# Two thirds of one weight row sent through few partitions, one bias load, and four small operations on ScalarE, in a one-core decode kernel

## The chip, the cores and the metric

The kernel runs on one core of a Trainium2 chip. The metric is the device time of one execution in microseconds (us). The time before is the median of three runs.

## What is computed

Two tokens (B = 2, one position each, D = 576) go through an attention block over a cached context and through a dense MLP, and a sigmoid gate mixes the two results. Everything is fp32.

```python
B, Sq, D = 2, 1, 576;  H, Sk, Dh = 32, 4096, 128;  F = 4608
q = (x @ wq) per head
scores = einsum(q, k_cache) * Dh ** -0.5
o = softmax(scores) @ v_cache
a = o.reshape(B, Sq, H * Dh) @ wo
h = gelu(x @ w1 + b1);  b = h @ w2 + b2
g = sigmoid((x * gate_w).sum(-1))
out = g * a + (1 - g) * b
```

`k_cache` and `v_cache` are 134 MB each; the four weight matrices hold some 40 MB. All of it is read once.

## The kernel before, in words

**Storage.** One SBUF tile, `ring` (128 partitions x 49152 floats), takes every large transfer. It has three slots of 16384 floats. `wq` and `w1` come first and lie one behind the other from the start of the ring; behind them lie small temporaries. Then come, slot after slot, K and V of sixteen units (a unit is four heads of one token: 128 partitions x 64 KB), and then three groups of `w2` and `wo`, listed in `LAST` (lines 66 to 70). SyncE (SP) issues all of these in one order that is fixed in `seq` (lines 100 to 104); `load()` and `load_next()` issue the next one when its slot is free. A transfer over 128 partitions is cut into one piece for each partition.

**Start.** SP issues `wq` and `w1` (L119). ScalarE (ACT) issues the MLP's bias `b1` (L218), the two rows of `x` (L223) and `gate_w` (L224), and later `b2` (L314). TensorE transposes `x` (L270), makes the gate (L279) and the projection by `wq` (L303). ACT copies the projection to SBUF (L313), and TensorE gathers the heads (L328); then the first slot is free for the first K (L130). `q_unit` (L343) spreads the queries of four units over 128 partitions with POOL (L347), TensorE (L351) and ACT (L353).

**The MLP's hidden layer.** `w1`'s projection (L303 again) leaves token 0 and token 1 in rows 0 and 1 of each group of 32 partitions. `b1` is loaded twice, once for each of the two rows, by `load_b1`: for token 0 in one transfer ahead of `x`, for token 1 in five transfers behind `b2` (L315), each over 4 partitions. It is added ahead of the transpose (L390). GELU follows, and `hg` (128 partitions x 36 rows x 2 tokens) holds the result times the gate.

**The sixteen units.** VectorE (DVE) multiplies K by the query in place (L506) and sums over the head's 128 elements (L511, L512, with POOL adding halves in L510); the softmax runs on ACT (L531), and TensorE multiplies by V (L545). `keep` and `combine` (L556, L562) collect the results in `oall`.

**The end.** Row r of `w2` on partition p is row 36p + r of the matrix, and row r of `wo` on partition p is 32p + r. `mlp_out` and `wo_out` multiply row after row into one PSUM tile, `acc`, which has two halves of 288 columns (DS) for each of two parities of the row (`acc_mm`, L363). One half of `w2`'s last row, r = 35, is handled apart: its columns 288 to 575 are not in the transfer over 128 partitions (L158). They come as "wx", in four transfers over 4 partitions each (L155), so that 16 partitions hold 8 pieces each, one for each of the 128 places. `hx` holds the matching 128 values of `hg` in that layout (made by eight matmuls, L411, and one copy, L415), and `mlp_x` (L417) multiplies them. The wx transfers are issued between `w2` and `wo`. `wo` comes in pieces of 8, 8, 7, 4, 3, 1 and 1 rows, the last row in three parts (L166). After row 22 `acc` is copied to SBUF (L446); the rows from 23 on go to a second PSUM tile, `res` (L457, L481), in four column quarters, and `fold` adds the copied sums (L467). DVE and ACT copy `res` to SBUF (L477, L486), and SP writes the output (L487).

Between the last attention product and `wo_out` stands a short chain: the sum of the softmax weights (L570), reciprocal, the sum over `oall` and a scaling (L572 to L575, DVE), a transpose (L579, TensorE) and its copy (L580, DVE), `o_turn`'s transposes (L433, DVE), its matmul (L435) and its copy `oP` (L436, DVE).

What orders the DMAs: SP issues in program order. A transfer waits for its slot's readers. The framework also has eight semaphores that the transfers of SP and ACT take in turn, so that a transfer waits until the eighth one before it has landed.

## Time and profile before

| what | value |
|---|---|
| median of 3 runs | 721.74 us (721.65 to 721.84) |
| the profiled execution | 721.61 us |
| its span, from first to last instruction | 719.7 us |
| read from HBM | 308.59 MB, 429 GB/s over the span |
| granted TensorE clock, mean | 0.658 |
| DVE, PE, POOL, ACT busy | 511.8, 216.2, 145.0, 40.0 us |

The profile comes from one execution, 0.13 us below the median of the runs. Its times are us from the start of the span. The profiled time is 1.9 us above the span; that part lies outside what the trace shows. "PE" is TensorE's matmuls, "PEld" its weight loads; "SPq" and "ACTq" are DMA issues by SyncE and ScalarE. In the rows by windows, the two last columns are the share of the 16 DMA engines' time that packets took, and GB/s. A packet is counted whole in the window in which it starts, so a short window can show a share above 1. In the rows of DMA queues, q1 is what SP issues, q10 what ACT issues, and q8 and q14 are instruction fetches; the columns are packets, MB, and share of the 16 engines' time in the window.

### The profile page before, as it was taken

To read this page: it belongs to the slowest core of one execution; us is meant where nothing else is said; L and a number is where in the kernel's file an instruction comes from. 1 tells how busy PE (TensorE), PEld (TensorE's weight loads), DVE (VectorE), ACT (ScalarE), POOL (GpSimd) and SP (SyncE) were. 2 spreads that over 40 slices of the span, in tenths; PEclk is the share of its full clock that TensorE was granted. 3 is DMA by queue.
4 is the path that set the end of the run, shared out by engine and by line. 5 is a ranking of instruction groups with operands and counts; after the bars stand their busy time and mean duration, and the time that the engine had idled before them with its cause. 6 is when DMAs were issued, how large, how long until landed. Compare 5 with 4: busy or idle time off the path is not lost.

```text
span 719.7 us, 3881 instructions
## 1 busy us (share of the span) xinstructions
PE 216.2 (30%) x1647; PEld 62.6 (9%) x1647; DVE 511.8 (71%) x136; ACT 40.0 (6%) x156; POOL 145.0 (20%) x35
## 2 busy tenths in 40 slices
PE   0665022040515050404032140505050503113195
PEld 0322000010101010101000010101010100000032
DVE  0004969779695969596969879696959695988910
ACT  0110010100001010101010100001010101010000
POOL 2000130404050403022040404040503122040400
PEclk9977556575756575566657575657575665757599
DMA  9999999999999999999999999999999999999997
GB/s 409 412 446 427 423 452 415 459 416 452 423 437 424 444 426 430 442 430 441 433 431 437 430 426 444 427 437 437 437 427 448 419 434 433 430 441 434 417 424 310
DMA packets 7278, 308.85 MB, mean 429 GB/s; under 512 B 830, under 2 KB 1362, under 8 KB 1628
## 3 DMA queue, kind: packets, MB, share of 16 engines
q1 hardware_dynamic: 7204, 308.55, 99.2%
q8 instruction: 13, 0.21, 0.1%
q10 hardware_dynamic: 56, 0.05, 0.0%
q14 instruction: 5, 0.04, 0.0%
HBM read 308.59 MB, written 0.00 MB: 429 GB/s over the span
## 4 chain that ended last, share of the span: by engine, by line
DMA 47%; DVE 35%; PE 15%; ACT 1%; issue 1%; ACTq 1%; POOL 0%; DVEq 0%; SPq 0%; POOLq 0%
DMA ring<-in_A_k_cache_dram 38%; DVE ring L506 19%; DVE s L511 10%; PE av L545 10%; DVE s L512 5%; DMA ring<-in_B_w_dram 4%; DMA ring<-in_A_wo_dram 3%; DMA ring<-in_gate_w_dram 3%; PE oall L562 2%; PE qps L303 2%; PE acc L367 1%; DVE avs L556 1%; ACTq L218 0%; PE qps L328 0%; ACT p L531 0%
## 5 line engine op out<-in xcount | busy, mean ns | idle before, releaser
L506 DVE TENSOR_TENSOR ring<-ring,q 128x16384 f32<-128x16384 f32 x16 | 275.6, 17225 | 109.1 <-DMA ring<-in_A_k_cache_dram 109.1
L510 POOL TENSOR_TENSOR ring<-ring 128x3968 f32<-128x3968 f32 x16 | 137.0, 8565 | 490.1 <-DVE ring L506 490.1
L545 PE MATMUL av<-ring,p 128*32 128x512 f32 x1024 | 137.5, 698 | 166.9 <-ACT p L531 166.9
L511 DVE TENSOR_REDUCE s<-ring 128x66 f32<-128x8448 f32 x16 | 143.3, 8953 | 1.3
L562 PE MATMUL oall<-avs,pick 128*64 128x512 f32 x16 | 14.8, 1028 | 196.7 <-DVE avs L556 168.3
L512 DVE TENSOR_REDUCE s<-ring 128x62 f32<-128x3968 f32 x16 | 68.4, 4277 | 0.1
L545 PEld LDWEIGHTS av<-ring,p 128*32 128x32 f32 x1024 | 35.1, 127 | 274.8 <-issue 217.8
L531 ACT ACTIVATE p<-s,bs 32x128 f32<-32x128 f32 x64 | 25.5, 398 | 478.9 <-DVE bs L525 477.7
L351 PE MATMUL qb<-qm,spread 64*128 64x512 f32 x8 | 8.3, 1138 | 72.5 <-POOL qm L347 72.5
L390 DVE TENSOR_TENSOR ring<-hps,ring 128x384 f32<-128x384 f32 x3 | 1.7, 559 | 33.3 <-PE hps L303 33.1
L562 PEld LDWEIGHTS oall<-avs,pick 128*64 128x64 f32 x16 | 2.2, 196 | 203.5 <-DVE avs L556 203.5
L367 PE MATMUL acc<-ring,hg 128*2 128x288 f32 x142 | 11.9, 487 | 26.1 <-DMA ring<-in_B_w_dram 26.1
L283 DVE TENSOR_SCALAR gb<-gb 128x2 f32<-128x2 f32 x1 | 0.2, 170 | 24.7 <-ACT gb L282 24.7
L556 DVE TENSOR_TENSOR avs<-av,selr 128x512 f32<-128x512 f32 x8 | 5.5, 682 | 10.6 <-PE av L545 10.6
L303 PE MATMUL hps<-ring 128*32 128x384 f32 x120 | 12.8, 598 | 0.0
L347 POOL TENSOR_TENSOR qm<-qall,mine 64x512 f32<-64x512 f32 x4 | 4.1, 1032 | 41.7 <-ACT qall L330 41.7
L477 DVE COPY ring<-res 2x144 f32<-2x144 f32 x1 | 0.3, 297 | 16.4 <-PE res L457 16.4
L531 ACT ACTIVATION_READ_ACCUMULATOR p<-s,bs 32x1 f32 x64 | 11.8, 184 | 0.0
L303 PE MATMUL qps<-ring 128*32 128x512 f32 x80 | 11.3, 729 | 0.0
L270 PE MATMUL xps<-ident,ring 3*128 3x3 f32 x10 | 1.5, 254 | 24.0 <-DMA ring<-in_gate_w_dram 23.1
L351 PEld LDWEIGHTS qb<-qm,spread 64*128 64x128 f32 x8 | 2.0, 307 | 75.6 <-POOL qm L347 75.6
L353 ACT COPY q<-qb 128x512 f32<-128x512 f32 x4 | 2.3, 586 | 106.3 <-PE qb L351 106.3
(87 smaller groups left out, 74.3 us busy)
## 6 DMA issues: line engine op xcount, KB each, us to landing
ring<-in_B_w_dram SPq DMA_DIRECT2D x2, 4608.0 KB, 34.4
ring<-in_B_w_dram SPq DMA_DIRECT2D x2, 4032.0 KB
ring<-in_A_wo_dram SPq DMA_DIRECT2D x2, 2304.0 KB, 14.9
ring<-in_B_w_dram SPq DMA_DIRECT2D x1, 2160.0 KB
ring<-in_A_wo_dram SPq DMA_DIRECT2D x1, 2016.0 KB
ring<-in_B_w_dram SPq DMA_DIRECT2D x1, 1152.0 KB, 14.7
ring<-in_A_wo_dram SPq DMA_DIRECT2D x1, 1152.0 KB
ring<-in_A_wq_dram SPq DMA_DIRECT2D x1, 1024.0 KB
```

The source lines that it names most:

```text
L303: nc.tensor.matmul(ps[32 * j:32 * j + 32, :width], lhs, ts[c][:, o:o + width], start=(k == 0), stop=last, skip_group_check=True,)
L347: nc.gpsimd.tensor_mul(t, qall.unsqueeze(1).to_broadcast([NO, NQ, DH]), mine[:, u[0]:u[-1] + 1].unsqueeze(2).to_broadcast([NO, NQ, DH]),)
L351: nc.tensor.matmul(ps, spread, t.rearrange("p u d -> p (u d)"), start=True, stop=True)
L367: nc.tensor.matmul(acc[o:o + m], lhsT, rhs[:, (s - lo) * DS:(s - lo + 1) * DS], start=start, stop=stop, skip_group_check=True)
L506: nc.vector.tensor_mul(kt[i], kt[i], qs[i].unsqueeze(1).to_broadcast([P, R, DH]))
L510: nc.gpsimd.tensor_add(t[:, :, :DH2], t[:, :, :DH2], t[:, :, DH2:])
L511: nc.vector.tensor_reduce(st[i][:, HALVED:], kt[i][:, HALVED:], AX.X, ALU.add)
L512: nc.vector.tensor_reduce(st[i][:, :HALVED], t[:, :, :DH2], AX.X, ALU.add)
L531: nc.scalar.activation(p[w, :, e * RB:(e + 1) * RB], st[i][w].rearrange("p (t c) -> p t c", c=RB), AF.Exp, bias=bias[i][w], accum_out=rs[w ...
L545: nc.tensor.matmul(ps[32 * j:32 * j + 32], p[:, 32 * t + EB * (1 - half):32 * t + EB * (1 - half) + 32], vt[i][:, RB * t:RB * (t + 1)].rea ...
L556: nc.vector.tensor_mul(t, avs[i].rearrange("p (r d) -> p r d", d=DH), selr.unsqueeze(2).to_broadcast([P, RB, DH]))
L562: nc.tensor.matmul(oall, pick[:, NO - G - i * G:2 * NO - G - i * G], avs[i].rearrange("p r d -> p (r d)"), start=(i == 0), stop=(i == N // ...
```

## The change

- **wx is wider and lies differently.** It takes 512 columns (64 to 575) of `w2`'s row 35 in place of 288, so that L158's transfer (now L166) has 224 columns less on each partition. Of the 128 places, 120 come in four transfers over 6 partitions with 5 places each (2 KB pieces), and the last 8 in a fifth transfer over 4 partitions with 2 places each.
- **`mlp_x`** has 7 steps in place of 8, and each has two matmuls (224 and 288 columns) in place of one of 288. `acc_mm` is written for any range of columns. `hx` is made in two parts (5 + 2 matmuls, two copies).
- **`wo` is cut** 7, 7, 9, 4, 3, 1, 1, since the second group has less room in its slot. The assertion is new, and checks that.
- **`b1` is loaded once**, in three transfers over 4 partitions, to row 2 of each group of 32, ahead of `x` on ACT's queue. The five transfers behind `b2` are gone. After the transpose one DVE addition adds that row to both tokens.
- **Four small operations go from DVE to ACT:** the copies of `spread`, `oT` and `oP`, and the scaling of `osum`.

```diff
-        (("w2", 28, 36), ("wx", 0, 1), ("wo", 0, 8), ("wo", 8, 16)),
-        (("wo", 16, 23), ("wo", 23, 27), ("wo", 27, 30), ("wo", 30, 31), ("wo", 31, 32)),
+        (("w2", 28, 36), ("wx", 0, 1), ("wo", 0, 7), ("wo", 7, 14)),
+        (("wo", 14, 23), ("wo", 23, 27), ("wo", 27, 30), ("wo", 30, 31), ("wo", 31, 32)),
...
-    XE, XC = 4, 4
+    XE, XC, XS, XW = 6, 4, 5, 512
     XP = XE * XC
-    XS = P // XP
-    srcx2 = w2.rearrange("(e c s r) n -> c r e s n", e=XE, c=XC, s=XS)[:, NF - 1, :, :, DS:]
+    XN = XP * XS
+    XR, XT = 4, (P - XN) // 4
+    XL = D - XW
+    srcw = w2.rearrange("(p r) n -> p r n", r=NF)[:, NF - 1, XL:]
+    srcx2 = srcw[:XN].rearrange("(e c s) n -> c e s n", e=XE, c=XC)
...
-                xt = t[:XP, o:o + XS * DS]
+                xt = t[:XP, o:o + XS * XW]
                 for c in range(XC):
                     nc.sync.dma_start(xt[c::XC].rearrange("e (s n) -> e s n", s=XS), srcx2[c])
+                o += XS * XW
+                yt = t[:XR, o:o + XT * XW].rearrange("p (s n) -> p s n", s=XT)
+                nc.sync.dma_start(yt, srcw[XN:].rearrange("(p s) n -> p s n", s=XT))
...
-    load_b1(0, (0, F4))
+    for m in range(FB):
+        nc.scalar.dma_start(
+            b1r.rearrange("(g q) n -> g q n", g=NG)[:, B, m * FC:(m + 1) * FC],
+            b1.rearrange("(g n) -> g n", g=NG)[:, m * FC:(m + 1) * FC],
+        )
...
-    load_b1(1, (0, 232, 464, 696, 928, F4))
...
-    nc.vector.tensor_copy(
+    nc.scalar.copy(
         spread.rearrange("p (e c) -> p e c", e=E), row4.unsqueeze(2).to_broadcast([NO, E, PE_])
     )
...
-    hb = ht[:, :, :B]
+    hb = temp(NF * B).rearrange("p (r b) -> p r b", b=B)
+    nc.vector.tensor_add(hb, ht[:, :, :B], ht[:, :, B:B + 1].to_broadcast([P, NF, B]))
...
     def mlp_x():
-        for s in range(XS):
-            acc_mm(hx[:, s], rows["wx"][:, s], s, lo=1)
+        for s in range(XS + XT):
+            acc_mm(hx[s], rows["wx"][s], s, lo=XL)
...
-        nc.vector.tensor_copy(oP.rearrange("p b c -> p (b c)"), ps)
+        nc.scalar.copy(oP.rearrange("p b c -> p (b c)"), ps)
...
-        nc.vector.tensor_scalar_mul(osum, osum, f[:, 0:1])
+        nc.scalar.mul(osum, osum, f[:, 0:1])
```

Where the order of instructions moves, on SP at the end of the program. The rows are transfers, `in_B_w_dram` being `w2`, with their shape and what the issue waits for; a wait named DMAHW is for an earlier transfer's landing. Before:

```order
L158 DMA ring<-in_B_w_dram 128x4320 [waits DMAHW5_49,DVE_49]
L155 DMA ring<-in_B_w_dram 4x8x288 [waits DMAHW6_49]
L155 DMA ring<-in_B_w_dram 4x8x288 x3
L166 DMA ring<-in_A_wo_dram 128x4608
L166 DMA ring<-in_A_wo_dram 128x4608 [waits DMAHW7_49]
L166 DMA ring<-in_A_wo_dram 128x4032 [waits DMAHW0_49,PE_49]
L166 DMA ring<-in_A_wo_dram 128x2304 [waits DMAHW1_49,PE_49]
L166 DMA ring<-in_A_wo_dram 128x1728 [waits DMAHW2_49,PE_49]
```

And after, the same stretch:

```order
L166 DMA ring<-in_B_w_dram 128x4096 [waits DMAHW2_49,DVE_49]
L157 DMA ring<-in_B_w_dram 6x5x512 x4
L160 DMA ring<-in_B_w_dram 4x2x512 [waits DMAHW3_49]
L174 DMA ring<-in_A_wo_dram 128x4032 [waits DMAHW4_49]
L174 DMA ring<-in_A_wo_dram 128x4032 [waits DMAHW5_49]
L174 DMA ring<-in_A_wo_dram 128x5184 [waits DMAHW6_49,PE_49]
L174 DMA ring<-in_A_wo_dram 128x2304 [waits DMAHW7_49,PE_49]
L174 DMA ring<-in_A_wo_dram 128x1728 [waits DMAHW0_49,PE_49]
```

With one transfer more ahead of them, each of the `wo` transfers waits for the landing of the transfer eight before it, and that is now one later in the list of `w2` than before: the second piece waits for rows 14 to 27 of `w2`, and the third for rows 28 to 35.

On ACT at the start of the program, its first twelve rows, up to the second copy of the projection (L313, now L319) and what follows it. `in_B_b_dram` is `b1` in the rows with 4 partitions and `b2` in the row 1x576. Before (the next two rows are the last of the five `b1` transfers and the copies at L322):

```order
L218 DMA ring<-in_B_b_dram 4x1152
L223 DMA ring<-in_A_x_dram 1x576 x2
L224 DMA ring<-in_gate_w_dram 1x576
L261 ACT_TABLE_LOAD
L261 COPY ring<-ring 3x64 x2
L273 COPY ring<-xps 128x10x2
L275 COPY ring<-xps 128x5
L282 ACTIVATE gb<-zps 128x2
L313 COPY ring<-qps_150 128x512
L313 COPY ring<-qps_151 128x512
L314 DMA ring<-in_B_b_dram 1x576
L218 DMA ring<-in_B_b_dram 4x232 x4
```

After:

```order
L224 DMA ring<-in_B_b_dram 4x384 x3
L229 DMA ring<-in_A_x_dram 1x576 x2
L230 DMA ring<-in_gate_w_dram 1x576
L267 ACT_TABLE_LOAD
L267 COPY ring<-ring 3x64 x2
L279 COPY ring<-xps 128x10x2
L281 COPY ring<-xps 128x5
L288 ACTIVATE gb<-zps 128x2
L319 COPY ring<-qps_152 128x512
L319 COPY ring<-qps_153 128x512
L320 DMA ring<-in_B_b_dram 1x576
L327 COPY ring<-ident 128x4x2 x8
```

Two transfers more stand ahead of `x` and `gate_w`, and five fewer ahead of the copies at L322 (now L327).

## The prediction

> **What bounds the kernel now.** I begin with the page: is any engine full? DVE is busy for 71% of the span, the DMA engines for all of it, and the rows of the queues say what they carry.

> ```profile
> DMA  9999999999999999999999999999999999999997
> q1 hardware_dynamic: 7204, 308.55, 99.2%
> q8 instruction: 13, 0.21, 0.1%
> ```

> The DMA view for the first 710 us alone gives a sharper figure, and the rows by windows show that no stage is an exception:

> ```profile
> q1 hardware_dynamic: 6394, 306.44, 99.8%
> ...
> 2.00:36.00 34.00, 11.51 (x72) 5.55 (x76) 1.75 (x9) 2.09 (x6) 2.47 (x8) 1.00 0.96 413
> 36.00:45.75 9.75, 6.46 (x52) 3.33 (x40) 0.00 (x0) 2.07 (x10) 0.00 (x0) 0.88 0.98 422
> 110.00:650.00 540.00, 139.63 (x912) 34.08 (x904) 437.92 (x91) 29.18 (x115) 122.88 (x17) 0.62 1.00 433
> 690.00:712.00 22.00, 17.79 (x229) 6.35 (x223) 2.64 (x9) 0.43 (x1) 0.00 (x0) 1.00 1.00 425
> ```

> So SP's transfers keep all 16 engines at work from the start to 710 us. At 425 GB/s and share 1.00 one engine moves 26.6 GB/s. The long waits of the chain (K landing, 38% of the span) are this one limit seen from DVE. What is left to ask is how the work is spread over the 16 engines, since the last one to finish sets the end. The windows at the end answer that:

> ```profile
> 713.00:713.50 0.50, 0.19 (x8) 0.18 (x12) 0.00 (x0) 0.13 (x1) 0.00 (x0) 1.00 0.99 394
> 713.50:714.00 0.50, 0.50 (x24) 0.44 (x20) 0.00 (x0) 0.00 (x0) 0.00 (x0) 1.00 0.95 374
> 714.00:714.50 0.50, 0.50 (x24) 0.35 (x16) 0.00 (x0) 0.00 (x0) 0.00 (x0) 1.00 0.78 303
> 714.50:715.00 0.50, 0.22 (x8) 0.00 (x0) 0.00 (x0) 0.00 (x0) 0.00 (x0) 1.00 0.59 214
> 715.00:715.50 0.50, 0.14 (x8) 0.13 (x11) 0.00 (x0) 0.00 (x0) 0.00 (x0) 1.00 0.52 194
> 715.50:716.00 0.50, 0.50 (x24) 0.40 (x16) 0.00 (x0) 0.00 (x0) 0.00 (x0) 1.00 0.46 158
> 716.00:716.50 0.50, 0.50 (x22) 0.17 (x12) 0.00 (x0) 0.00 (x0) 0.00 (x0) 1.00 0.47 119
> 716.50:717.00 0.50, 0.50 (x15) 0.24 (x12) 0.10 (x1) 0.06 (x1) 0.00 (x0) 1.00 0.00 0
> ```

> The engines do not end together. At 713.5 all work; by 715 the share is 0.52, so eight (0.52 x 16) are through; the other eight run on to about 716.5. That is a spread of some 3 us. The chain of waits confirms that this decides:

> ```profile
> 695.27 20.04 DMA ring<-in_A_wo_dram
> ...
> 715.36 1.56 PE res L457 x36
> 716.92 0.28 DVE ring L477
> ```

> From 695 us on the chain is a `wo` transfer until 715.3, complete only when its slowest engine is, and then 1.56 us of matmuls. The pieces after it land on the same slow engines. **The step to cost is therefore: by how much does the slowest of 16 engines move?**

> **The change, part by part.** *The w2 row over 128 partitions.* Each partition has 224 columns, 896 bytes, less. An engine serves 8 of the 128 partitions, so each has 7168 bytes less: 0.27 us at 26.6 GB/s.

> *wx.* Before, four transfers bring 128 pieces of 1152 bytes; on four engines, as the four partitions suggest, that is 32 x 1152 = 36864 bytes each. After, if six partitions mean six engines, each of these gets 4 x 5 pieces of 2048 bytes = 40960, and four of them 2 pieces more = 45056. So per engine: the four old ones 45056 - 36864 - 7168 = +1024 bytes, 0.04 us, which ten packets fewer may take back: 0. Two new ones +33792 bytes: 1.27 us at 26.6 GB/s, or 1.57 at the 21.5 that a busy engine still makes of the small last pieces (158 GB/s at share 0.46); I take 1.3, as 2 KB pieces are longer than those. The other ten: -0.27.

> [...]

> *b1.* The five transfers behind `b2` disappear; at the start 4608 bytes for each of four partitions come as before, in three pieces. ACT's queue in the window that holds the five, and instruction fetches for comparison, here one in a window of 1 us:

> ```profile
> q10 hardware_dynamic: 41, 0.02, 1.1%
> ...
> q8 instruction: 1, 0.02, 6.3%
> ```

> 1.1% of 16 engines over the 6 us from 44 to 50 is 1.06 us for the 41 packets, `b2`'s included, so at most 0.26 us on each of four engines; less the two additional pieces at the start I take 0.2. As the queue never empties, an engine that is relieved at 45 us is still ahead at 716.

> The other row prices one fetch of 16 KB: 6.3% x 16 x 1.0 us = 1.0 us on one engine. Thirteen of them over a few engines make engines late that have nothing to do with wx. Of the eight late ones four are explained by wx and the rest by these.

> *ACT at the start.* These rows of the timeline tell when things are needed:

> ```profile
> 23.07 0.60 PE L270 MATMUL xps<-ident,ring 3*128 3x3 f32 x4 [23.07 <-DMA ring<-in_gate_w_dram]
> 39.79 2.65 ACTq L218 DMA_DIRECT2D ring<-in_B_b_dram  x5
> 42.74 3.01 PE L328 MATMUL qps<-ring 128*64 128x128 f32 x16 [3.29 <-ACT ring L322]
> 45.75 0.33 SPq L130 DMA_DIRECT2D ring<-in_A_k_cache_dram  x1
> ```

> `gate_w` lands fourth in ACT's queue at 23.0 and will land sixth. The first four took 21 us, some 5 each, because each of their packets takes its turn behind a 64 KB piece of `wq`; those pieces end at about 22 us (8 x 64 KB at 26.6 GB/s are 19.7 us, begun at 2), and 8 KB pieces follow. So the two transfers more cost 1 to 2 us, at most 10.5. Against that, 2.65 us of issues leave the path between the projection and L328. The first K would be issued about 1 us earlier than 45.75. Nor is it urgent: `wq` and `w1` are 20.05 MB, of which at 45.75 some 1.9 MB are still to come (34 us at 413 GB/s and 9.75 at 422 have passed), over 4 us of work. Cost 0.

> *GELU's addition and hx.* One DVE addition (0.2 us) delays `hg` and the K that waits for it at 69 us, while a whole V (8.4 MB, 19 us at 433 GB/s) is still queued ahead of it: 0.

> *SP at the end.*

> ```profile
> 681.76 0.33 SPq L158 DMA_DIRECT2D ring<-in_B_w_dram  x1
> 685.40 15.23 SPq L166 DMA_DIRECT2D ring<-in_A_wo_dram  x9
> ```

> wx is issued between these rows, four transfers in 2.8 us; a fifth makes `wo`'s first piece 0.7 us later. The second piece then waits for `w2`'s rows 14 to 27 and the third for rows 28 to 35, which land near 690 and 695 us. By 695 the first two `wo` pieces, 14 rows or 4.1 MB, are still queued: 9.7 us of cover. What the fifth could hold up is the `wo` issues behind it on SP, and none is due. Cost 0.

> *PE and the moved operations.*

> ```profile
> L575 DVE TENSOR_SCALAR ring<-ring 64x128 f32<-64x128 f32 x1 | 0.3, 277 | 0.0
> L580 DVE COPY oT<-oT_t 128x64 f32<-128x64 f32 x1 | 0.2, 225 | 1.5 <-PE oT_t L579 1.5
> L436 DVE COPY oP<-op_t 128x64 f32<-128x64 f32 x1 | 0.2, 224 | 1.8 <-PE op_t L435 1.8
> ...
> 705.82 2.12 PE L367 MATMUL acc<-ring,oP 128*2 128x288 f32 x32 [1.58 <-DMA ring<-in_A_wo_dram]
> 710.57 2.11 PE L367 MATMUL acc<-ring,oP 128*2 128x288 f32 x28 [2.63 <-DMA ring<-in_A_wo_dram]
> 713.31 1.16 PE L457 MATMUL res<-ring,oP 128*2 128x144 f32 x32 [0.63 <-DMA ring<-in_A_wo_dram]
> 715.36 1.51 PE L457 MATMUL res<-ring,oP 128*2 128x144 f32 x36 [0.64 <-DMA ring<-in_A_wo_dram]
> ```

> If ACT took twice as long for each of the three, that is 0.7 us, against 1.58 us in which PE sits waiting for `wo` afterwards; `spread` is covered by POOL's 1 us of L347. `mlp_x` goes from 16 to 28 matmul passes, under 1 us more at the 2.1 us that 16 took, in the same cover; if both bounds came together, 0.1 us would spill into the next gap of 2.63. The piece that lands at 710.5 now has 9 rows, not 7: 8 passes more at 2.11/28 = 0.6 us, which just fills the 0.63 at 713.31, with 0.64 more at 715.36. Cost 0; if the cover were gone, 0.6.

> **Sum.** The late engines: those of wx get 0.2 us less (b1), the others 0.27 less. All `wo` landings of the slowest engine move by about -0.25 us, and what follows them stays. The profiled 721.61 us become 721.36; the median, 0.13 above it, 721.74 becomes 721.5. That is -0.03%. The measurement tells 0.2% from no change, 1.44 us, so this counts as the same.

> **The rivals.**
> 1. *The relief doesn't arrive.* The windows show when engines finish, not which, and a fetch of 1 us can fall on another engine, since PE's program changes by a few instructions. Then 721.7. Chance 0.13.
> 2. *An additional wx engine is one of the late ones.* It adds 1.3 us to an engine that is at most 0.3 us ahead of the last: 722.7 to 723.0. Of the 12 engines without wx, eight are early and four late; knowing no more, both new ones are early with 8/12 x 7/11 = 0.42. But following the packets by hand through the records, end to start (no view lists them by engine), the q8 fetches come back to the same engines and spare those of wx and the early ones beside them. [...] Chance of the rival 0.12.
> 3. *Slower: six partitions don't give six engines.* If the transfers went over two, each would get 4 x 3 x 5 x 2048 = 122880 bytes, 86016 more than before: 3.2 us less 0.27. If those two are among the late, the end is at 724.6; it decides once an engine gets more than the 3 us of spread. For it: no such shape in the trace. Against: four partitions evidently use more than two. Chance 0.03.
> 4. *Slower: `x` late.* If the two transfers cost 10.5 us, the first K comes 7.9 us later, the queue is empty for 3.5, and nothing gives that back: 725.2. It decides from 7 us on (4.4 of cover and 2.65 saved). Against: the 8 KB pieces. Chance 0.03.
> 5. *Each transfer has a fixed price.* If engines idled for an issue (0.7 us), the fifth would cost that: 722.4. Against, q1's row for 692 to 694.25 us, in which wx passes:

> ```profile
> q1 hardware_dynamic: 202, 1.00, 106.9%
> ```

> The engines stay full. Chance 0.02. [...]

> **How the numbers follow.** Forecast 0.67, at 721.5. With rivals 1, 2 and 5 the chance within 721.1 to 722.9 is over 0.9 before my own errors; I keep that range, the lower end being the forecast less 0.4 (both reliefs on one engine). Slower by over 0.2% (above 723.18): rivals 3 and 4 and the upper end of 2, 0.08. Faster by over 0.2% (below 720.30): the idle shares of the windows from 713.5 to 716.5 add up to 1.1 us an engine (0.5 x (0.05 + 0.22 + 0.41 + 0.48 + 0.54 + 0.53)), so even a perfect spread does not reach that: 0.02. Same: 0.90.

> **What would show it.** Right: q1 still 99.8% until 710 us; the first K issued before 46 us; the share of the last windows falling later and more steeply, with nearly nothing after 716.3; L457's last group starting near 715.1. Wrong: an empty stretch near 50 us (rival 4); a share of one or two engines after 716.8 (2, 3); PE waiting nowhere after 713 us (then PE sets the end).

## The result and the profile after

The changed kernel took 723.20 us (median of 13 executions, 722.12 to 724.46), the kernel before 721.57 beside it (13 executions, 721.31 to 721.84). The ratio is 1.0023, with a 95% interval of 1.0015 to 1.0032. The forecast was 721.5, with a range up to 722.9: the change makes the kernel slower by about 1.6 us, and the median lies outside the range. The fastest execution after is slower than the slowest before. The profiled execution of after took 722.87 us, 1.26 more than the profiled one of before.

First what came as forecast. The start of after, and its last transfers, in the timeline, the DMA view for the first 710 us, and the windows at the end:

```profile
24.02 0.61 PE L276 MATMUL xps<-ident,ring 3*128 3x3 f32 x4 [24.02 <-DMA ring<-in_gate_w_dram]
38.33 0.33 SPq L130 DMA_DIRECT2D ring<-in_A_k_cache_dram  x1
```

```profile
q1 hardware_dynamic: 6408, 306.42, 99.8%
```

```profile
714.50:715.00 0.50, 0.50 (x8) 0.13 (x2) 0.00 (x0) 0.00 (x0) 0.00 (x0) 0.50 0.73 271
715.50:716.00 0.50, 0.50 (x16) 0.29 (x14) 0.00 (x0) 0.17 (x1) 0.00 (x0) 0.51 0.52 166
716.00:716.50 0.50, 0.50 (x23) 0.38 (x21) 0.00 (x0) 0.00 (x0) 0.00 (x0) 1.00 0.12 36
716.50:717.00 0.50, 0.50 (x28) 0.40 (x22) 0.00 (x0) 0.00 (x0) 0.00 (x0) 1.00 0.16 33
```

`gate_w` lands 1 us later, the first K is issued before 46, the queue is as full as ever, and the last transfers end earlier: between 716.0 and 716.5 there are 36 GB/s where before had 119. The 33 GB/s of the last row are 16 KB in half a microsecond, an instruction fetch. In this execution, then, the engines are better balanced, as the forecast said.

Now the chain that ended last, and TensorE's timeline:

```profile
694.62 15.60 DMA ring<-in_A_wo_dram
710.26 4.25 PE acc L375 x33
...
715.23 1.30 PE res L469 x19
...
718.17 0.28 DVE ring L489
```

```profile
702.66 3.58 PE L375 MATMUL acc<-ring,oP 128*2 128x288 f32 x44
710.26 4.49 PE L375 MATMUL acc<-ring,oP 128*2 128x288 f32 x34 [4.02 <-DMA ring<-in_A_wo_dram]
```

In before the chain's last DMA step reached to 715.3; now it ends at 710.26, and from there TensorE itself is the end. It waited 4.02 us for the nine-row piece (before: 2.63 us for the seven rows), and then never again. The columns of the windows that explain it are PE's busy time, the first number behind the window's length, and PEclk, the third number from the right:

```profile
685.00:686.00 1.00, 1.00 (x20) 0.43 (x16) 0.00 (x0) 0.00 (x0) 0.00 (x0) 0.86 1.19 516
...
706.00:707.00 1.00, 0.24 (x2) 0.00 (x0) 0.00 (x0) 0.00 (x0) 0.00 (x0) 1.00 1.09 454
707.00:708.00 1.00, 0.00 (x0) 0.00 (x0) 0.00 (x0) 0.00 (x0) 0.00 (x0) 1.00 0.92 394
708.00:709.00 1.00, 0.00 (x0) 0.00 (x0) 0.00 (x0) 0.00 (x0) 0.00 (x0) 1.00 0.96 410
709.00:710.00 1.00, 0.00 (x0) 0.00 (x0) 0.00 (x0) 0.00 (x0) 0.00 (x0) 0.58 0.87 366
710.00:711.00 1.00, 0.74 (x8) 0.26 (x12) 0.00 (x0) 0.00 (x0) 0.00 (x0) 0.50 1.02 433
...
715.00:716.00 1.00, 1.00 (x22) 0.56 (x22) 0.00 (x0) 0.40 (x1) 0.00 (x0) 0.50 0.59 202
716.00:717.00 1.00, 1.00 (x40) 0.77 (x38) 0.00 (x0) 0.00 (x0) 0.00 (x0) 1.00 0.14 34
```

Behind the idle stretch the granted clock falls to 0.50 and stays there until 716. The nine rows run from 710.26 to 715.23, 4.97 us for 36 records (0.14 each, three `res` records among them), against 2.11 / 28 = 0.075 in before. At the end of the chain DVE copies `res` at 718.17, in before at 716.92: 1.25 us later, and the profiled executions differ by 1.26. One execution is thus accounted for. Whether it is typical, and which part of the change does it, the experiments have to say.

### The profile page after: what moved, and what is told of

Its sections match the earlier page's. It is cut to its first block, busy times and chain, and to the rows that moved or that the text cites. A ratio compares the mean times of both kernels' runs of the same rounds, so it can differ in the third digit from the quotient of the medians.

```text
span 721.1 us, 3896 instructions
## 1 busy us (share of the span) xinstructions
PE 215.6 (30%) x1657; PEld 62.7 (9%) x1657; DVE 511.0 (71%) x133; ACT 41.0 (6%) x161; POOL 145.0 (20%) x35
## 3 DMA queue, kind: packets, MB, share of 16 engines
q1 hardware_dynamic: 7216, 308.55, 99.0%
## 4 chain that ended last, share of the span: by engine, by line
DMA 47%; DVE 35%; PE 14%; ACT 2%; issue 1%; ACTq 0%; POOL 0%; DVEq 0%; SPq 0%; POOLq 0%
DMA ring<-in_A_k_cache_dram 40%; DVE ring L518 19%; DVE s L523 10%; PE av L557 9%; DVE s L524 5%; DMA ring<-in_gate_w_dram 3%; DMA ring<-in_A_wo_dram 2%; ACT p L543 2%; DMA ring<-in_B_w_dram 2%; PE hps L309 2%; PE qps L309 2%; DMA ring<-in_B_b_dram 1%; PE acc L375 1%; PE res L469 0%; PE zps L285 0%
## 5 line engine op out<-in xcount | busy, mean ns | idle before, releaser
L375 PE MATMUL acc<-ring,hg 128*2 128x288 f32 (+1 forms) x142 | 11.9, 484 | 26.1 <-DMA ring<-in_B_w_dram 26.1
L489 DVE COPY ring<-res 2x144 f32<-2x144 f32 x1 | 0.3, 296 | 19.7 <-PE res L469 19.7
L309 PE MATMUL hps<-ring 128*32 128x384 f32 x120 | 12.7, 591 | 0.0
L309 PE MATMUL qps<-ring 128*32 128x512 f32 x80 | 10.9, 705 | 0.0
L375 PE MATMUL acc<-ring,oP 128*2 128x288 f32 x92 | 9.5, 513 | 4.0 <-DMA ring<-in_A_wo_dram 4.0
```

The source lines that it names most:

```text
L309: nc.tensor.matmul(ps[32 * j:32 * j + 32, :width], lhs, ts[c][:, o:o + width], start=(k == 0), stop=last, skip_group_check=True,)
L375: nc.tensor.matmul(acc[o:o + m, u - s * DS:v - s * DS], lhsT, rhs[:, u - lo:v - lo], start=start, stop=stop, skip_group_check=True,)
```

## The experiments

**The theories.** A: the cut of `wo` into 7, 7, 9 rows lengthens TensorE's wait before the last large piece; a wait that long lets the granted clock fall, and the nine rows run at half rate. Rivals: B, the wide wx, the bias or the moved operations make the loss; C, nine rows are too much work behind the transfer whatever the clock; D, a transfer lands late in some executions; E, more transfers at the end, issued later, are the loss by themselves. "Fillers" are matmuls whose result nobody reads. All ratios below are against the kernel before, run beside each set.

**1. The cut alone, in the old kernel.**

```
-(("w2", 28, 36), ("wx", 0, 1), ("wo", 0, 8), ("wo", 8, 16)),
-(("wo", 16, 23), ("wo", 23, 27), ...
+(("w2", 28, 36), ("wx", 0, 1), ("wo", 0, 7), ("wo", 7, 14)),
+(("wo", 14, 23), ("wo", 23, 27), ...
```

> The kernel before, with nothing changed but the cut of wo: 7, 7, 9, 4, 3, 1, 1 rows in place of 8, 8, 7, 4, 3, 1, 1. Theory A (the cut alone makes the loss: TensorE idles about 4 us ahead of the 9-row piece, its granted clock falls to 0.5, and the matmuls become the end): 722.6 to 724.0 us, clock near 0.5 from about 710 to 715, runs spread over more than 1 us. Theory B (the loss comes with the wider wx, the bias or the operations moved to ScalarE): 721.3 to 721.8, clock 1.00 to the end.

Measured: 722.68 us, ratio 1.0012 (1.0003 to 1.0021), and not one cloud but two: five of 11 executions at 721.59 to 722.00, six at 722.68 to 723.24. TensorE's timeline, and windows:

```profile
710.52 3.77 PE L367 MATMUL acc<-ring,oP 128*2 128x288 f32 x34 [4.01 <-DMA ring<-in_A_wo_dram]
```

```profile
683.00:684.00 1.00, 1.00 (x16) 0.33 (x12) 0.00 (x0) 0.95 (x5) 0.00 (x0) 0.51 1.12 484
...
711.00:712.00 1.00, 1.00 (x16) 0.39 (x12) 0.00 (x0) 0.00 (x0) 0.00 (x0) 0.64 1.00 424
...
714.00:715.00 1.00, 1.00 (x21) 0.48 (x16) 0.00 (x0) 0.18 (x1) 0.00 (x0) 0.65 0.75 288
```

The same wait, the same fall of the clock, without wx, bias or moved operations: the cut makes a loss by itself. Here the clock is low for 3.4 us only, and this execution ends at about 721.9; the upper group has no trace.

**2. The nine rows split again, in the new kernel** (`("wo", 14, 23)` becomes `("wo", 14, 19), ("wo", 19, 23)`), twice.

> The changed kernel with the 9-row piece of wo in two transfers, 5 and 4 rows. Theory A: the 5 rows land about 2.8 us before the 4, TensorE's longest idle time falls to some 2 us, the clock stays at 1.00, and the time is the one that the DMA engines give, 721.1 to 721.5 us, runs within 0.5 us of each other. Theory B: 722.6 to 723.8, as changed.

> The changed kernel with the 9-row piece as 5 and 4 rows once more, one execution, for a second trace: its executions fell into two groups, near 721.9 and from 722.7 to 724.2 us. Theory A (clock): if this one is slow, the clock shows 0.5 in some stretch after 695 us, and the last wo landing is no later than in a quick one (717.0). Theory D (DMA): if slow, the clock is 1.00 and the last landing is 1 us later, since an instruction fetch has fallen on an engine that carries wx.

Measured: 722.68 us, ratio 1.0013 (1.0004 to 1.0022); 0.5 us better than the new kernel, but again two groups, five at 721.82 to 722.04 and six at 722.68 to 724.23, where I had expected one. The trace of the first run (721.82 us) shows a clock of 1.00 to the end. The second execution that was traced took 722.06 us, and in it the clock falls although no wait behind 703 us is longer than 1.58 us. The rows of the first run's first `res` group, of the second's, and windows of the second:

```profile
713.45 1.16 PE L469 MATMUL res<-ring,oP 128*2 128x144 f32 x32 [1.61 <-DMA ring<-in_A_wo_dram]
```

```profile
713.25 2.10 PE L469 MATMUL res<-ring,oP 128*2 128x144 f32 x32 [1.58 <-DMA ring<-in_A_wo_dram]
```

```profile
710.00:711.00 1.00, 0.49 (x10) 0.22 (x13) 0.00 (x0) 0.00 (x0) 0.00 (x0) 1.00 1.03 435
711.00:712.00 1.00, 0.66 (x12) 0.10 (x4) 0.00 (x0) 0.27 (x1) 0.00 (x0) 1.00 0.97 408
712.00:713.00 1.00, 0.00 (x0) 0.00 (x0) 0.00 (x0) 0.13 (x1) 0.00 (x0) 0.99 0.95 390
713.00:714.00 1.00, 0.75 (x16) 0.48 (x20) 0.00 (x0) 0.00 (x0) 0.00 (x0) 0.50 0.93 377
```

The same 32 records take 2.10 us in place of 1.16. So it is not the length of one wait that counts but, as it seems, how much TensorE works in a stretch, here 1.15 us of the 3.4 before 713; the last section counts that over all traces. At 722.06 us this execution lies below the upper group, so a fall as late as this one does not make an upper time by itself.

**3. The gap filled, too much,** and **the cut 7, 8, 8,** both in the new kernel.

```
 wo_out(0, 14)
+warm = ps_sm.tile([B, DS], F32, tag="sm", name="warm")
+for _ in range(10):
+    nc.tensor.matmul(warm, oP[:, :, 0], rows["wo", 0][:, :DS], start=True, stop=True)
 wo_out(14, FOLD)
```

> The changed kernel with ten matmuls more between row 13 and row 14 of wo, into a PSUM tile that nothing reads; the 9-row piece stays. Theory A: the idle time shrinks from 4.0 to under 2.5 us, the clock stays at 1.00, nine rows take 2.7 us in place of 5, 721.1 to 721.6 us. Theory C (nine rows behind one landing are too much work for the end whatever the clock): 722.0 to 723.5.

> The changed kernel with wo cut 7, 8, 8, which still fits the slots. Theory A: TensorE works on 8 rows from the second piece until about 707.1 us and then idles some 3.1 us, between the 2.6 that kept the clock and the 4.0 that lost it: 721.1 to 721.6 us if 3.1 us are still short enough, 722.3 or more, with a spread, if not. Theory B: 722.6 to 723.8.

Measured with ten fillers: 722.74 us, ratio 1.0010 (1.0001 to 1.0019); five at 721.50 to 721.70, six at 722.74 to 723.69. They took 0.48 us each, 4.8 in all, more than the gap, so this run doesn't decide. With 7, 8, 8: 722.93 us, ratio 1.0019 (1.0010 to 1.0027), spread over 721.56 to 724.20; its traced execution (721.93 us) waited 3.33 us and kept its clock.

**4. The other parts, each on the old kernel:** the bias once and four operations on ACT; the wide wx with the split cut 7, 7, 5, 4; the split cut alone.

> The kernel before with the bias loaded once and the four operations on ScalarE; wx and the cut of wo as before. Theory A and theory D: 721.3 to 721.7 us, all executions within 0.8 us, since neither the cut nor wx changes. Theory B (the bias or the moved operations): a second group of executions at 722.7 or above.

> The kernel before with the wide wx and wo cut 7, 7, 5, 4; bias twice, the four operations on VectorE. Theory A (the cut is mended): 721.2 to 721.9 us, one group. Theory D (wx on six engines): two groups, as with everything changed, median 722.3 or above. Theory B: one group, as A.

> The kernel before with wo cut 7, 7, 5, 4, 4, 3, 1, 1 and nothing else. Theory A and theory D: 721.3 to 721.9 us, one group. Theory E (more transfers at the end, or the later issue of the wo pieces behind earlier landings, whatever wx and the clock): two groups, median above 722.

Measured: 722.14 us for the bias and the operations, ratio 1.0006 (0.9997 to 1.0015, which holds 1), all 11 executions between 721.84 and 722.37, so half a microsecond later than forecast. Its trace says that the transfers are late, by 0.5 us at the third `wo` piece (before: 710.57):

```profile
711.08 3.21 PE L364 MATMUL acc<-ring,oP 128*2 128x288 f32 x28 [2.66 <-DMA ring<-in_A_wo_dram]
```

The 28 records take 3.21 us instead of 2.11, so the clock fell in this execution of the old cut too (0.50 in the windows from 712 to 715 us); here the 1.1 us stay within the 1.27 us of waiting behind the piece.

The wide wx with the split cut: 722.75 us, ratio 1.0010 (1.0001 to 1.0019), two groups: four at 721.50 to 721.76, one at 722.23, six at 722.75 to 722.97. The split cut with the old wx: 721.78 us, ratio 1.0004 (0.9995 to 1.0013), nine of 11 below 722.1. So E falls, and the upper group comes with the wide wx; theory A has nothing to say to it. There are two causes, then.

**5. Fillers of the right number:** six after row 13 (four after row 15 in the old kernel, with the old cut), 0.48 us each.

> The new kernel with six matmuls of no use (out of 2x288, results never read, about 2.9 us in all) in TensorE's stream between wo's row 13 and the nine-row piece. Theory A (a stretch of one clock window with TensorE mostly idle halves the granted clock for the nine rows): the granted clock stays at 1.00 to the end, TensorE idles under 2.2 us in one piece after 703 us, and the runs form one group at 721.2 to 721.8 us, all of the 1.6 us won back although no transfer and no row has moved. Theory C (nine rows are too much work whatever the clock) and B or D (the wide wx, the bias loaded once, the late ScalarE operations or a late transfer): still 722.5 to 723.3.

> The old kernel with the cut 7, 7, 9 alone, which had two groups, around 721.8 and around 722.9 us, and the same six matmuls of no use after row 13. Theory A: the upper group is gone, one group at 721.4 to 721.9, the clock 1.00 to the end. C or D: two groups as before, median above 722.3.

> The old kernel with the wide wx and the cut 7, 7, 9, its bias still loaded twice and its late operations where they were, and the six matmuls of no use. Theory A with the bias term at 0 to +0.3: 721.1 to 721.6, one group, last wo transfer 0.2 to 0.3 us earlier than before; this would be the fastest version. If the wide wx or the nine rows cost by themselves: above 722.

> The old kernel unchanged but for four of the matmuls of no use (1.9 us) after wo's row 15, in its idle stretch of 2.63 us: what they cost by themselves, and whether the old kernel too loses a little to the clock in some runs. Theory A: 721.3 to 721.7, with fewer runs above 721.8 than without them; no run slower for them. If the matmuls of no use cost time or hold a transfer back: 722 and more, and the kernels with six of them have to be read less that cost.

| kernel | median | ratio (interval) | executions |
|---|---|---|---|
| new, six fillers | 722.12 | 1.0009 (1.0000 to 1.0018) | 5 at 721.57 to 721.88, 2 at 722.1, 4 at 722.76 to 723.15 |
| old, cut 7, 7, 9, six fillers | 721.67 | 1.0008 (0.9993 to 1.0023) | 10 at 721.36 to 721.87, one apart at 727.62 |
| old, wide wx, cut 7, 7, 9, six fillers | 721.57 | 1.0005 (0.9996 to 1.0014) | 7 at 721.37 to 721.81, 4 at 722.70 to 722.92 |
| old, four fillers | 721.52 | 0.9999 (0.9990 to 1.0008) | 11 at 721.41 to 721.98 |

(Executions of the kernel before stood apart as well, in other sets: one at 729.09, one at 888.41. The 727.62 and the 729.09 show a mean granted clock of 0.60 and 0.57, the rest of their sets 0.65 to 0.67.) The second row is the clearest: the nine rows, the same transfers, and more work for TensorE, and the upper group of experiment 1 is gone. Its timeline shows why, a wait of 1.57 us where there were 4.01, and the nine rows at full rate:

```profile
706.23 2.83 PE L625 MATMUL warm<-ring,oP 128*2 128x288 f32 x11
710.62 2.60 PE L367 MATMUL acc<-ring,oP 128*2 128x288 f32 x36 [1.57 <-DMA ring<-in_A_wo_dram]
713.36 1.16 PE L457 MATMUL res<-ring,oP 128*2 128x144 f32 x32
```

C falls with it: at the full clock the nine rows end at 713.22 (710.62 + 2.60), just before the next transfer lands at 713.36, as the forecast had it. In the new kernel the fillers win back 1.1 us of the 1.6, where I had expected all of it. What is left is again an upper group, in both kernels with the wide wx and in neither with the old one.

**6. The upper group of the wide wx.** wx over twelve partitions (`XE, XC, XS, XW = 12, 2, 5, 512`), and four single executions with a trace of kernels with wx over six, to catch one of the upper group.

> The old kernel with the wide wx, the cut 7, 7, 9 and six fillers, but the 120 places of wx in two transfers over 12 partitions in place of four over 6: if partitions mean engines, twelve engines get 20480 bytes each (0.77 us at 26.6 GB/s) where six had 40960 (1.54 us). If an engine that has both wx and the instruction fetches makes the upper group: the upper group comes down by about 0.77 us, to 721.9 to 722.2, and the lower one stays or falls by up to 0.5; but more engines carry some of wx, so more executions may be of the upper group. If the clock makes it: two groups as before, 721.5 and 722.8.

> The same kernel as the one with the wide wx, the new cut and six fillers, for its trace. If it falls into the upper group (some 4 in 10): by rival 2 the last wo transfer lands about 1.2 us later than in the lower group (near 717.8 instead of 716.6 on the trace's scale), with the clock at 1.00 to the end; by the clock theory the landing is unchanged and the clock falls to 0.50 after 706 us.

> As the second look: about 721.5 us with TensorE's last group starting near 715.2, or about 722.8 us; then by rival 2 that group starts near 716.4 with the clock at 1.00, by the clock theory it starts near 715.2 to 716 with the clock at 0.50.

> The old kernel with the wide wx and the cut 7, 7, 5, 4, looked at again for the trace of its upper group (6 of 11 executions at 722.75 to 722.97 us, 4 at 721.5 to 721.8). In the upper group, by rival 2 (a new wx engine is late): TensorE's last group starts 1.2 us later, near 716.4, the clock 1.00 to the end. By the clock theory: a stretch of 3.4 us at 0.50 behind 706 us. In the lower group near 721.6 us with neither.

> As the second look: 721.6 us, or near 722.8 us with either a last group of TensorE that starts near 716.4 at a clock of 1.00 (rival 2) or a stretch of 3.4 us at a clock of 0.50 (clock theory).

Measured: the four single executions took 721.49, 721.61, 722.21 and 721.51 us. None is of the upper group; the third is one more fall of the clock (0.50 from 713.2 on, behind waits of 1.30, 1.11 and 1.57 us). Twelve partitions: 723.89 us, ratio 1.0032 (1.0020 to 1.0044), all six executions at 723.32 to 724.79, with a clock of 1.00 in the trace. I had expected at most 722.2 and was wrong. Windows of the twelve and, behind them, of the first of the four single executions, with wx over six:

```profile
692.00:693.00 1.00, 1.00 (x21) 0.28 (x12) 0.48 (x1) 0.00 (x0) 0.00 (x0) 1.00 0.97 267
695.00:696.00 1.00, 1.00 (x24) 0.42 (x16) 0.74 (x2) 0.00 (x0) 0.00 (x0) 1.00 1.08 271
```

```profile
692.00:693.00 1.00, 1.00 (x16) 0.26 (x12) 0.00 (x0) 0.00 (x0) 0.00 (x0) 1.00 1.02 419
```

The engines are as busy but move a third less: the 2 KB packets, by the trace's records 84 ns each over six partitions, take 113 on average over twelve. So this run brought in a new cost and does not tell how the upper group arises. One kernel was left for that: take away nearly all that TensorE has to do behind the transfers, so that a slow clock has nothing to stretch.

```
-wo_out(14, FOLD)
+wo_out(FOLD - 1, FOLD)
...
-for r in range(FOLD, 31):
+for r in (FOLD, FOLD + 3):
```

> The old kernel with the wide wx, the cut 7, 7, 9 and six fillers, but the matmuls of wo's rows 14 to 21, 24, 25 and 27 to 30 are left out, their transfers kept: 44 records of TensorE's work in place of 112 after the nine-row transfer, and behind the last transfer only row 31, some 0.5 us. Its output is therefore not the reference's. Rival 2 (the last transfer is late in some executions, whatever TensorE does): two groups as with all rows, near 721.4 and 722.7, about 4 in 11 in the upper one. Clock theory (a slow clock stretches TensorE's work behind the transfers): one group at 721.2 to 721.8, as half a clock costs at most 0.3 us on what is left.

Measured: 723.00 us, ratio 1.0006 (0.9986 to 1.0026, with the 729.09 among the executions of before); three executions at 721.64 to 721.82, eight at 722.66 to 723.24. Two groups with at most 0.3 us left to stretch: they are the transfers' own. The traced execution (723.09 us) is of the upper group. Its timeline and windows, and then those of the kernel with all rows in its lower group (721.45 us):

```profile
717.72 0.65 PE L471 MATMUL res<-ring,oP 128*2 128x144 f32 x4 [2.25 <-DMA ring<-in_A_wo_dram]
```

```profile
716.00:717.00 1.00, 0.00 (x0) 0.00 (x0) 0.00 (x0) 0.00 (x0) 0.00 (x0) 0.55 0.15 49
717.00:718.00 1.00, 0.28 (x6) 0.15 (x8) 0.00 (x0) 0.00 (x0) 0.00 (x0) 0.50 0.05 17
```

```profile
716.56 0.51 PE L495 MATMUL res<-ring,oP 128*2 128x72 f32 x8
```

```profile
716.00:717.00 1.00, 1.00 (x28) 0.36 (x19) 0.25 (x1) 0.21 (x1) 0.00 (x0) 1.00 0.16 47
717.00:718.00 1.00, 0.07 (x3) 0.00 (x0) 0.35 (x2) 0.34 (x2) 0.00 (x0) 1.00 0.00 0
```

Between 717 and 718 the share is 0.05, which is 0.8 of one engine: a single engine still works, and TensorE starts on the last row 1.2 us or more later (717.72 behind a wait, against 716.56 at the latest without one).

The records of the trace, which no view lists, say which engine it is. For each transfer over 128 partitions they have 16 times at which its semaphore is counted up, which I take as one for each engine, and for each of the first four wx transfers, besides one at the issue, six. In the first part of the last row (the transfer of 1152 bytes for each partition) the last engine is 4.7 us behind the first of the 16, the next one 3.5; in the other 19 traces the last engine is 2.9 to 3.5 behind there. In this trace the last engine had been 3.1 behind before wx, one of two so late, and wx added the rest: one chain of 20 wx packets begins at 694.06 us, those of the other five between 691.6 and 692.8. That chain is through at 696.03, and the fifth wx transfer with its four engines before it, at 695.13; so its engine is none of the four that the fifth uses. In the 12 other traces with wx over six partitions all six are through with their 20 packets by 694.9. If those four are the engines that wx had before, which no run shows, this is my rival 2, an additional wx engine that is one of the late ones; it rests on the trace of one upper execution. The low clock of the last rows can add at most some 0.3 us here.

## Why the prediction was wrong

*What held.* The slowest engine moves by -0.25 us: in the traced execution the last transfers end about that much earlier (0.27 by the semaphores). Six partitions give six engines: wx shows as six chains of packets in the records, and each of its first four transfers is counted up six times, so rival 3 is out. That the four engines of the old wx are among the six, by which the forecast has 0 for them and 1.3 us for two new ones, no run shows; what the runs showed are the six counts and the end 0.27 us earlier. `x` and `gate_w` cost 1 us (the records show the packets of ACT's queue 2.4 to 2.6 us apart up to 22 us in both traces, about as long as a 64 KB packet of `wq` takes, 2.50 us on average, and 0.3 to 0.4 apart behind that in after), and the first K is not late for it (rival 4): it is issued 7.4 us earlier rather than 1, since SP's wait for it now ends with the projection (L309), and as the queue was full anyway nothing came of that. The issues on SP at the end cost nothing that the share shows (rival 5): q1 has 109.4% from 692 to 694.25 us, in before 106.9%. `mlp_x` takes 2.10 us as before, with 28 passes in place of 16. ("Under 1 us more" does not follow from the prediction's own figures, by which 12 passes more are 12 x 2.1 / 16 = 1.6 us; no such time was added.)

*The step that failed.* It is the one on TensorE: "8 passes more at 2.11/28 = 0.6 us, which just fills the 0.63 at 713.31 ... Cost 0; if the cover were gone, 0.6." The step priced the nine rows with the duration of a record at the full clock, and looked only at the gaps behind them. The change also takes two rows away ahead of the piece, so that TensorE is through with them at 706.24 in place of 707.94, and the gap before the piece grows from 2.63 to 4.02 us. That I had not worked out. At half clock the nine rows take 4.97 us, where the seven took 2.11: 2.86 more. (At the full clock they take 2.60, by experiment 5: 0.5 more, as the step had it, which the cover takes in.) The piece lands 0.31 earlier (710.26 against 710.57) and 1.27 us of waiting lay behind it (0.63 + 0.64), so 2.86 - 0.31 - 1.27 = 1.28 us pass on to the end. Measured there: 1.25. By medians over all executions, the fillers, which touch nothing else, give back 1.1 us. The text named the sign: "PE waiting nowhere after 713 us (then PE sets the end)". That is what the trace shows.

*A chance that was far too small.* Rival 2 had its price right (722.7 to 723.0 forecast, 722.7 to 723.2 measured), and its mechanism as far as the one trace of an upper execution shows it, but a chance of 0.12. In the six kernels of this study with wx over six partitions and either the split cut or fillers, 34 of 66 timed executions lie above 722.6 (a clock that falls may have a part in those of the split cut). With the old wx and the same tails it is one of 21 (the split cut, the six fillers), the execution at 727.62 left out. I had followed the fetches through the packets of a single trace and put the two new engines among the early ones, though no run shows which engines the six are; in the traced upper execution one of the six is late, in the other 12 traces none. Whether the fetches make it late, and what decides on which engines they fall, stays open: no view numbers the engines, and none of these runs moves the fetches alone. Where the lower and the upper group are about equally frequent, one trace can't tell the odds.

*A term of the wrong sign.* The bias loaded once, forecast at -0.2 us, was +0.5 with the four operations on ACT in the old kernel (722.14 against 721.59). Beside fillers, the lower groups differ by about 0.2 (721.57 to 721.88 with them, 721.37 to 721.81 without). Where it begins can be read from the traces. SP's three issues of `w1` in before and in after, at the start of the program (the first number is the start of the first, the second the time until the last is through):

```profile
1.63 34.75 SPq L119 DMA_DIRECT2D ring<-in_B_w_dram  x3
```

```profile
22.65 1.28 SPq L119 DMA_DIRECT2D ring<-in_B_w_dram  x3
```

With two transfers more on ACT's queue the semaphores come round earlier, and SP issues `w1`'s first piece only when `wq`'s first has landed (at 22.63 us); the part on ACT at the start looked at `gate_w` alone. In the seven traces with the bias loaded once, the first engine is through with that piece at 35.55 to 35.69 us, in the other 13 at 35.29 to 35.46, and some 0.2 us of this is still there at the first piece of `w2` (677.04 to 677.43 against 676.76 to 677.11). So this part of the loss is older than any of the four operations on ACT. That the later issue makes it, and where the rest of the 0.5 comes from, is not shown: neither was tried alone.

The three don't simply add up: a late transfer gives TensorE time to catch up (in experiment 4, 1.1 us of lost clock stayed within 1.27 us of waiting). The traces show each of them; how they combine in the 13 executions of the new kernel, of which only one was traced, stays open, and so does why none of them is below 722.12, where five of 11 with the cut alone are. No version beats the kernel before by more than the measurement can tell: the lower group with the wide wx (721.37 to 721.81) is at best 0.1 us below it, and it is only about half of the executions.

## What to carry to other kernels

Where a change moves work from one side of a wait to the other, work out the wait on both sides, and price the matmuls behind a long wait at the clock that will be granted there (here 0.50 behind 4.02 us, 4.97 us for nine rows in place of 2.60), not at the one that the trace of before shows. When the end is set by the slowest of several engines, one trace shows one draw: look at the spread of the executions, and at several traces, before calling an engine early. A few matmuls of no use in a known gap are a cheap test for a clock loss; in the kernel before, four of them cost nothing that the measurement can tell (0.9999, 0.9990 to 1.0008).

## What the runs showed of the hardware

*The busy share of such a window tells the falls from the rest in these traces.* In the window that ended with a fall TensorE worked 14% (after: 705.75 to 709.16, work until 706.24), 22% (experiment 1: 707.87 to 711.28, work from 710.52) and 34% (split cut: 1.15 of 3.41 us) of the time. In the trace of the cut 7, 8, 8 the window from 705.88 to 709.29 had 43% (work until 707.35), and the clock stayed:

```profile
685.00:686.00 1.00, 1.00 (x20) 0.34 (x14) 0.00 (x0) 0.16 (x2) 0.00 (x0) 0.80 1.04 452
...
707.00:708.00 1.00, 0.35 (x8) 0.00 (x0) 0.00 (x0) 0.00 (x0) 0.00 (x0) 1.00 0.99 424
```

The bound lies between 34% and 43% as far as these four go. The records of all 20 traces, cut into the windows of each trace's own grid, narrow it: from 60 us on, the 331 windows that ended with a fall were busy for at most 40.6%, and the 723 at whose end the full rate stayed for at least 40.8%. (Before 60 us, where TensorE does the short matmuls of the start, four windows of 45% to 71% ended with a fall too.) Waits of at most 1.58 us were enough for a fall (split cut). Back to full rate it came after one full window in experiment 1 (711.28 to 714.70), and in after only after the second; the first (709.16 to 712.57) was 68% busy. Over all traces from 60 us on, no window under 77% brought the full rate back and every one over 83% did.

*The 2 KB packets were slower over twelve partitions:* they went from 84 to 113 ns on average, and the core from 419 to 267 GB/s for a window, when each wx transfer went over twelve partitions in place of six. What makes them slower was not tried.
